# Attention and a gated network on one core: scores computed once with the queries on the partitions, probabilities transposed by TensorE, and an instruction order fixed by a list schedule

## The chip, the cores and the metric

The kernel runs on one core of a Trainium2 chip. The metric is the device time of one execution in microseconds (us). Engines are named as in the profile: PE is TensorE's matmul, PEld its weight load, DVE is VectorE, ACT is ScalarE, POOL is GpSimd, SP is the queue that issues the DMAs.

## The reference

Four batches of eight heads, 1152 keys, 64 columns a head. Neighbouring queries are averaged in pairs, which leaves 576. The heads of a batch are joined to 512 columns and go through a gated network of width 1536.

```python
q_pool = q.reshape(B, H, S // 2, 2, D).mean(axis=3)       # 4, 8, 576, 64
scores = scale * np.matmul(q_pool, k.transpose(0, 1, 3, 2))
attn = np.exp(scores - scores.max(-1, keepdims=True))
attn = attn / (attn.sum(-1, keepdims=True) + 1e-09)
x = np.matmul(attn, v)       # then (B * 576, 512)
gate = 1.0 / (1.0 + np.exp(-(x @ w_gate)))
out = (gate * (x @ w_val)) @ w_out
```

The network's weights are 64-bit floats; the kernel reads them as pairs of 32-bit words and converts them itself.

## The kernel before

To keep the accuracy of fp32 at the speed of TensorE's fp32r type, a factor is split into a rounded high half and the rest, the low half. A product is then three matmuls (high x high, high x low, low x high) that add up in PSUM; for the scores, k's halves and q's halves are stacked on the 128 partitions, 64 each, so that two matmuls do (`KA` with `QA` at L226, `KB` with `QB` at L228).

The scores are computed twice. `nat_chunk` (L186) puts the queries on the partitions and takes the maximum of each query over 384 keys at a time (L195). `aug` (L199) joins the maxima and writes them as diagonals into `QB` (L211), so that the second score pass subtracts them. That second pass, `scores` (L217), puts the keys on the partitions: for each head nine slots of 128 keys by 576 queries, cut into 256 and 320 columns (`CUT`, L28). ACT takes the exponential (L232), and the result is already the way round that the product with v needs. From head 18 on (`SPLIT`) the probabilities are split: the high half by ACT (L237), the low half by DVE (`p_lo`, L240), and the product with v is four matmuls a slot (`av`, L247); before that, v and the probabilities go in as plain fp32, with ones beside v that give the denominators. For split heads POOL adds up the exponentials (L275), and `den` (L303) sums over partitions by matmul. `av_evac`, `recip` and `norm` (L277 to L338) combine the halves, divide, and split the result x into `xh` and `xl`.

The network (`groups`, L419) is cut into thirds of the width. A group is one PSUM tile of 256 or 320 queries and 12 matmuls: 512 columns of x (L439) for the gate and the value, which give `gh` and `gl`, or 512 columns of these for the output (L469), summed into `opart`. Weights are converted once (`weight_piece`, L361, in DVE's L373, L374 and L380), split, stored in DRAM and loaded again for each batch.

Batch 0 is done in two units, first its 256, then its 320 queries, each with all eight heads; the other batches are one unit. The loop at L529 runs over slots: slot i issues the scores of i, the product with v of i - 2, and, once `ready` (L348) allows, one group of the network of the unit before. This order of the program and some priorities (`tc.high_priority`, `tc.issue_after`) go to a scheduler, which sets the order of each engine's instructions.

Of the kernel before, what the change touches and what calls it, by code (L numbers as in the profile page):

```python
# [12 lines left out]
ALU = mybir.AluOpType  # L13
PSUM = bass.MemoryType.PSUM
# [5 lines left out]

@with_exitstack
def attention_glu_kernel(ctx: ExitStack, tc: tile.TileContext, qT, kT, vt, v, wg, wv, wo, out):
# [3 lines left out]
    NC = SK // 128  # L26

    CUT = ((0, 256), (256, 576))  # L28
    FF_T = 12
    THIRDS = 3  # L30

    TURN = 15
    SPLIT = 18
    LAG = 4
    AHEAD = 2
    FIRST_W = 64

    units = [(0, (0,)), (0, (1,))] + [(b, (0, 1)) for b in range(1, B)]
    heads = [(b, ns, h) for b, ns in units for h in range(H)]
    NU = len(heads)  # L40
    NSLOT = NU * NC

    const = ctx.enter_context(tc.tile_pool(name="const", bufs=1))
    vt_p = ctx.enter_context(tc.tile_pool(name="vt", bufs=2))
    e_p = ctx.enter_context(tc.tile_pool(name="e", bufs=3))
    y_p = ctx.enter_context(tc.tile_pool(name="y", bufs=2))
    one_p = ctx.enter_context(tc.tile_pool(name="one", bufs=1))
    x_p = ctx.enter_context(tc.tile_pool(name="x", bufs=7))
    g_p = ctx.enter_context(tc.tile_pool(name="g", bufs=4))
    sg_p = ctx.enter_context(tc.tile_pool(name="sg", bufs=2))  # L50
    w_p = ctx.enter_context(tc.tile_pool(name="w", bufs=2))
    dr_p = ctx.enter_context(tc.tile_pool(name="dr", bufs=1, space=DRAM))
    ps_s = ctx.enter_context(tc.tile_pool(name="ps_s", bufs=4, space=PSUM))
    ps_a = ctx.enter_context(tc.tile_pool(name="ps_a", bufs=1, space=PSUM))
    ps_m = ctx.enter_context(tc.tile_pool(name="ps_m", bufs=2, space=PSUM))


    early = ctx.enter_context(ExitStack())
    pools = {"raw": early.enter_context(tc.tile_pool(name="raw0", bufs=2))}
    set_p = early.enter_context(tc.tile_pool(name="set0", bufs=1))  # L60

    def late_pools():
        early.close()
        pools["raw"] = ctx.enter_context(tc.tile_pool(name="raw", bufs=1))
        pools["pp"] = ctx.enter_context(tc.tile_pool(name="pp", bufs=3))
        pools["acc"] = ctx.enter_context(tc.tile_pool(name="acc", bufs=2))


    ident2 = const.tile([128, 64], F32, name="ident2")
    ones_r = const.tile([128, 192], F32R, name="ones_r")  # L70

    sets = (const, const, set_p)
    KA = [p.tile([128, SK], F32R, name=f"KA{i}") for i, p in enumerate(sets)]
    KB = [p.tile([128, SK], F32R, name=f"KB{i}") for i, p in enumerate(sets)]
    QA = [p.tile([128, SQ + 64], F32R, name=f"QA{i}") for i, p in enumerate(sets)]
    QB = [p.tile([128, SQ + 64], F32R, name=f"QB{i}") for i, p in enumerate(sets)]
    opart = [const.tile([128, SQ], F32, name=f"opart{i}") for i in range(4)]

    blk = [ones_r[:, 64:192], ones_r[:, 0:128]]

    w_d = {
        "g": dr_p.tile([FF_T, 128, 2, 2, 512], F32, name="wg_d"),
        "o": dr_p.tile([THIRDS * 4, 128, 2, 1, 512], F32, name="wo_d"),
    }

    st = {}

    def op(u):

        return u % 3 if u <= TURN else (u - TURN) % 2  # L90

    def after(u):

        if u < TURN:
            return u + 2
        return u + 1 if TURN < u < NU - 1 else None

    def split(u):
        return u >= SPLIT

    def whole(u):
        return len(heads[u][1]) == 2

    def span(u):
        ns = heads[u][1]
        return CUT[ns[0]][0], CUT[ns[-1]][1]

    def row(u):
        return heads[u][0] * H + heads[u][2]

    def less(to_vector):

        return nc.vector if to_vector else nc.gpsimd


    def load_kq(u):
        a, b = span(u)
        t = pools["raw"].tile([128, SK], F32, tag="kraw", name="kraw")
        r = pools["raw"].tile([128, 2, SQ], F32, tag="qraw", name="qraw")
        for p in (slice(0, 64), slice(64, 128)):  # L120
            nc.sync.dma_start(out=r[p, :, a:b], in_=qT[row(u)][:, :, a:b])
            nc.sync.dma_start(out=t[p], in_=kT[row(u)])
        st["kraw", u] = t
        st["qraw", u] = r

    def load_v(u):
        if split(u):
            t = pools["raw"].tile([128, NC, D], F32, tag="vraw", name="vraw")
            nc.sync.dma_start(out=t, in_=v[row(u)])
            st["vraw", u] = t  # L130
        else:

            t = vt_p.tile([128, 2, D * NC], F32, tag="vt", name="vo")
            nc.gpsimd.memset(t[:, 1 - u % 2], 1.0)
            nc.sync.dma_start(out=t[:, u % 2], in_=vt[row(u)])
            st["vt", u] = t.rearrange("p a (d c) -> p c (a d)", c=NC)


    def prep_k_hi(u):
        for s in (slice(0, SQ), slice(SQ, SK)):  # L140
            nc.scalar.activation(out=KA[op(u)][:, s], in_=st["kraw", u][:, s], func=ACTF.Copy)  # L141

    def prep_k_lo(u, part):
        s = slice(part * SQ, part * SQ + SQ)
        nc.gpsimd.tensor_tensor(  # L145
            out=KB[op(u)][64:128, s], in0=st["kraw", u][64:128, s],
            in1=KA[op(u)][64:128, s].bitcast(F32), op=ALU.subtract,
        )

    def prep_qs(u):  # L150
        a, b = span(u)
        t = pools["raw"].tile([128, SQ], F32, tag="qs", name="qs")
        qr = st.pop(("qraw", u))
        less(u == 1).tensor_tensor(out=t[:, a:b], in0=qr[:, 0, a:b], in1=qr[:, 1, a:b], op=ALU.add)
        st["qs", u] = t

    def prep_q_hi(u):
        a, b = span(u)
        for p, q in ((slice(64, 128), QB[op(u)]), (slice(0, 64), QA[op(u)])):
            nc.scalar.activation(out=q[p, a:b], in_=st["qs", u][p, a:b], func=ACTF.Copy)  # L160

    def prep_q_lo(u):
        a, b = span(u)
        less(heads[u][0] == 1).tensor_tensor(
            out=QA[op(u)][64:128, a:b], in0=st.pop(("qs", u))[64:128, a:b],
            in1=QB[op(u)][64:128, a:b].bitcast(F32), op=ALU.subtract,
        )

    def prep_v(u):
        if not split(u):  # L170
            return
        t = vt_p.tile([128, NC, 2 * D], F32R, tag="vt", name="vt")
        vr = st.pop(("vraw", u))
        nc.scalar.activation(out=t[:, :, 0:D], in_=vr, func=ACTF.Copy)
        nc.gpsimd.tensor_tensor(
            out=t[:, :, D:2 * D], in0=vr, in1=t[:, :, 0:D].bitcast(F32), op=ALU.subtract
        )
        st["vt", u] = t


    def nat_list(u):
        a, b = span(u)
        return [(t, j) for t in range(a // 128, (b + 127) // 128) for j in range(3)]

    def nat_chunk(u, t, j):
        if ("pm", u) not in st:  # L186
            st["pm", u] = y_p.tile([128, 5, 3], F32, tag="pm", name="pm")
        ps = ps_s.tile([128, 512], F32, tag="s", name="nps")
        N = 384

        nc.tensor.matmul(  # L191
            out=ps[:, 0:N], lhsT=QA[op(u)][:, t * 128:(t + 1) * 128],
            rhs=KA[op(u)][:, j * N:(j + 1) * N], start=True, stop=True,
        )
        nc.vector.tensor_reduce(  # L195
            out=st["pm", u][:, t, j:j + 1], in_=ps[:, 0:N], axis=mybir.AxisListType.X, op=ALU.max
        )

    def aug(u):  # L199
        a, b = span(u)  # L200
        t0, t1 = a // 128, (b + 127) // 128
        nm = y_p.tile([128, 5], F32, tag="nm", name="nm")
        pm = st.pop(("pm", u))
        nc.vector.tensor_reduce(
            out=nm[:, t0:t1], in_=pm[:, t0:t1], axis=mybir.AxisListType.X, op=ALU.max, negate=True
        )
        q2 = QB[op(u)][0:64, 0:SQ].rearrange("p (a c) -> p a c", c=64)
        for par in range(2):
            p = slice(64 * par, 64 * par + 64)
            n = len(range(2 * t0 + par, b // 64, 2))  # L210
            nc.vector.tensor_tensor(  # L211
                out=q2[:, 2 * t0 + par:b // 64:2], in0=ident2[p].unsqueeze(1).to_broadcast([64, n, 64]),
                in1=nm[p, t0:t0 + n].unsqueeze(2).to_broadcast([64, n, 64]), op=ALU.mult,
            )


    def scores(i):  # L217
        u, c = divmod(i, NC)
        ks = slice(c * 128, (c + 1) * 128)
        e = e_p.tile([128, SQ], F32, tag="e", name="e")  # L220
        st["e", i] = e
# [41 lines left out]
    def acc_sum(i):  # L263
        u, c = divmod(i, NC)
        a, b = span(u)
        if c == 0:
            return
# [379 lines left out]
```

## Time and profile before

| | |
|---|---|
| median of three runs | 1094.63 us (1094.1 to 1097.09) |
| the profiled execution | 1094.97 us, span 1093.2 us |
| PE busy, PEld busy | 989.4 us (91%), 937.3 us (86%) |
| DVE busy | 863.4 us (79%) |
| ACT busy, POOL busy | 636.0 us (58%), 654.7 us (60%) |
| DMA moved | 173.38 MB, mean 159 GB/s |

Busy time is a sum over instructions. A matmul's time in flight overlaps the next one's, so a PE that is busy 91% need not be at its fastest; the distance between the starts of neighbouring matmuls shows how fast they go. An idle time counts only on the engine that sets the pace of its stage. The network's first matmul starts at 104.3 us, and the last matmul of all ends some 3.5 us before the end of the span. The span runs from the first to the last instruction; the execution's time has a little more around it.

### The profile page before, as it was taken

The page shows a single profiled execution, that of the slowest core. Times are in us where ns is not written, and L with a number is a line of the kernel's source. Part 1 is how long each engine was busy: PE and PEld are TensorE (multiplying, and loading weights), DVE is VectorE, ACT ScalarE, POOL GpSimd, SP SyncE. Part 2 cuts the span into 40 slices and gives each one's busy share as a digit, 9 for nine tenths or more (in the row PEclk, how much of TensorE's full clock was granted, in tenths as well). Part 3 has the DMA queues.
Part 4 walks back from the last instruction along what each step waited for, and adds up shares of the span by engine and source line. Part 5 has one row for each costly group of instructions (what it writes and reads, how often), then busy time and mean ns, then how long its engine had stood idle before and what let it go on. Part 6 is the DMA issues. An engine that isn't in the chain of part 4 may idle for free.

```text
span 1093.2 us, 17681 instructions
## 1 busy us (share of the span) xinstructions
PE 989.4 (91%) x6328; PEld 937.3 (86%) x6328; DVE 863.4 (79%) x1310; ACT 636.0 (58%) x1413; POOL 654.7 (60%) x461
## 2 busy tenths in 40 slices
PE   4999898989999888889898898899999898999998
PEld 3889887778999878879898898888898888999998
DVE  6877989968597998989889988889989988841222
ACT  3775656565665676666676655666676555632211
POOL 5774656444466787867698767768778665620000
PEclk9999999999999998989999998999999998999999
DMA  9974876776655544544544333454434331344443
GB/s 222 290 199 110 264 233 244 239 258 208 199 184 183 170 131 132 159 129 132 142 122 131 119 113 110 132 175 127 131 105 132 111 109 40 116 160 173 146 167 98
DMA packets 46040, 173.38 MB, mean 159 GB/s; under 512 B 6016, under 2 KB 11136, under 8 KB 38272
## 3 DMA queue, kind: packets, MB, share of 16 engines
q1 hardware_dynamic: 45952, 172.25, 50.9%
q8 instruction: 50, 0.82, 0.3%
q14 instruction: 38, 0.31, 0.1%
HBM read 148.64 MB, written 23.59 MB: 158 GB/s over the span
## 4 chain that ended last, share of the span: by engine, by line
PE 44%; DVE 37%; ACT 7%; DMA 6%; issue 5%; POOL 1%; SPq 1%; DVEq 0%; ACTq 0%; POOLq 0%
PE gps L439 14%; DVE pl L243 13%; PE ops L469 10%; PE avps L258 8%; DVE pm L195 8%; PE sps L226 4%; PE sps L228 4%; DVE QB L211 3%; DVE gl L453 3%; PE nps L191 3%; ACT e L232 2%; DMA wraw<-in_wg_dram 2%; ACT ph L237 2%; DVE hh L449 2%; DVE wraw L374 1%
## 5 line engine op out<-in xcount | busy, mean ns | idle before, releaser
L439 PE MATMUL gps<-xh,wg 128*128 128x320 f32 (+1 forms) x1536 | 342.8, 302 | 2.6 <-ACT xh L336 2.4
L232 ACT ACTIVATE e<-sps 128x256 f32<-128x256 f32 (+1 forms) x576 | 220.0, 406 | 181.7 <-PE sps L228 161.1
L243 DVE TENSOR_TENSOR pl<-e,ph 128x576 fp32r<-128x576 f32 x198 | 264.1, 1339 | 38.6 <-ACT ph L237 38.0
L275 POOL TENSOR_TENSOR acc<-acc,e 128x576 f32<-128x576 f32 x148 | 238.2, 1609 | 89.7 <-ACT e L232 84.3
L195 DVE TENSOR_REDUCE pm<-nps 128x1 f32<-128x384 f32 x480 | 246.2, 546 | 34.8 <-PE nps L191 33.2
L439 PEld LDWEIGHTS gps<-xh,wg 128*128 128x128 f32 x1536 | 262.9, 194 | 3.7 <-ACT xh L336 3.0
L439 PE MATMUL gps<-xl,wg 128*128 128x256 f32 (+1 forms) x768 | 231.3, 301 | 0.0
L226 PE MATMUL sps<-QA,KA 128*128 128x256 f32 (+1 forms) x576 | 190.4, 346 | 36.5 <-DVE pm L195 31.4
L145 POOL TENSOR_TENSOR KB<-kraw,KA 64x576 fp32r<-64x576 f32 x80 | 119.9, 1500 | 109.4 <-ACT KA L141 91.1
L228 PE MATMUL sps<-QB,KB 128*128 128x256 f32 (+1 forms) x576 | 168.9, 307 | 17.3 <-DVE QB L211 17.3
L469 PE MATMUL ops<-gh,wo 128*128 128x256 f32 (+1 forms) x768 | 171.8, 302 | 2.3 <-DMA wo<-wo_d 1.6
L191 PE MATMUL nps<-KA,QA 128*128 128x384 f32 x480 | 149.5, 381 | 23.9 <-ACT KA L141 8.7
L226 PEld LDWEIGHTS sps<-QA,KA 128*128 128x128 f32 x576 | 111.5, 195 | 55.3 <-DVE pm L195 47.2
L439 PEld LDWEIGHTS gps<-xl,wg 128*128 128x128 f32 x768 | 149.1, 194 | 0.6
L237 ACT ACTIVATE ph<-e 128x576 fp32r<-128x576 f32 x198 | 135.9, 688 | 11.1 <-PE avps L258 6.3
L258 PE MATMUL avps<-e,vo 128*128 128x256 f32 (+1 forms) x360 | 136.5, 467 | 3.3 <-ACT e L232 2.3
L469 PEld LDWEIGHTS ops<-gh,wo 128*128 128x128 f32 x768 | 131.7, 194 | 3.5 <-DVE opart L480 2.0
L228 PEld LDWEIGHTS sps<-QB,KB 128*128 128x128 f32 x576 | 110.9, 196 | 24.8 <-DVE QB L211 18.6
L191 PEld LDWEIGHTS nps<-KA,QA 128*128 128x128 f32 x480 | 87.3, 197 | 35.3 <-DVE pm L195 13.2
L469 PE MATMUL ops<-gl,wo 128*128 128x256 f32 (+1 forms) x384 | 115.6, 301 | 1.6 <-DVE gl L453 1.6
L258 PEld LDWEIGHTS avps<-e,vo 128*128 128x128 f32 x360 | 100.0, 326 | 6.9 <-ACT e L232 4.4
L258 PE MATMUL avps<-pl,vt 128*128 128x256 f32 (+1 forms) x396 | 93.6, 304 | 11.7 <-DVE pl L243 11.2
(65 smaller groups left out, 1374.9 us busy)
## 6 DMA issues: line engine op xcount, KB each, us to landing
wg<-wg_d SPq DMA_DIRECT2D x48, 1024.0 KB, 4.8
wo<-wo_d SPq DMA_DIRECT2D x48, 512.0 KB, 3.3
kraw<-in_kT_dram SPq DMA_DIRECT2D x80, 288.0 KB, 4.7
qraw<-in_qT_dram SPq DMA_DIRECT2D x48, 288.0 KB, 4.7
wg_d<-wg SPq DMA_DIRECT2D x12, 1024.0 KB, 5.2
vraw<-in_v_dram SPq DMA_DIRECT2D x22, 288.0 KB, 3.6
wraw<-in_wg_dram SPq DMA_DIRECT2D x12, 512.0 KB, 5.7
wraw<-in_wv_dram SPq DMA_DIRECT2D x12, 512.0 KB, 4.9
```

The source lines that it names most:

```text
L145: nc.gpsimd.tensor_tensor(out=KB[op(u)][64:128, s], in0=st["kraw", u][64:128, s], in1=KA[op(u)][64:128, s].bitcast(F32), op=ALU.subtract,)
L191: nc.tensor.matmul(out=ps[:, 0:N], lhsT=QA[op(u)][:, t * 128:(t + 1) * 128], rhs=KA[op(u)][:, j * N:(j + 1) * N], start=True, stop=True,)
L195: nc.vector.tensor_reduce(out=st["pm", u][:, t, j:j + 1], in_=ps[:, 0:N], axis=mybir.AxisListType.X, op=ALU.max)
L226: nc.tensor.matmul(out=ps[:, 0:b - a], lhsT=KA[op(u)][:, ks], rhs=QA[op(u)][:, a:b], start=True, stop=False)
L228: st["pace"] = nc.tensor.matmul(out=ps[:, 0:b - a], lhsT=KB[op(u)][:, ks], rhs=QB[op(u)][:, a:b], start=False, stop=True)
L232: nc.scalar.activation(out=e[:, a:b], in_=ps[:, 0:b - a], func=ACTF.Exp, scale=1.0 / 16.0)
L237: nc.scalar.activation(out=t[:, a:b], in_=st["e", i][:, a:b], func=ACTF.Copy)
L243: nc.vector.tensor_tensor(out=t[:, a:b], in0=st["e", i][:, a:b], in1=st["ph", i][:, a:b].bitcast(F32), op=ALU.subtract)
L258: nc.tensor.matmul(out=ps[:, 0:b - a], lhsT=st["vt", u][:, c], rhs=s[:, a:b], start=(c == 0 and k == 0), stop=(c == NC - 1 and k == len(sr ...
L275: eng.tensor_tensor(out=t[:, a:b], in0=t[:, a:b], in1=st["e", i][:, a:b], op=ALU.add)
L439: nc.tensor.matmul(out=ps[:, 0:N], lhsT=w[:, hl, s, kc], rhs=x, start=(kc == 0 and j == 0), stop=(kc == 3 and j == 2),)
L469: nc.tensor.matmul(out=ps[:, 0:N], lhsT=w[:, hl, 0, i], rhs=x[:, qc], start=(i == 0 and j == 0), stop=(i == 3 and j == 2),)
```

## The change

Almost all of the kernel's body is replaced; the inputs, the outputs and the splitting in halves stay.

- Scores are computed once, with the queries on the partitions, over all 1152 keys: a step is 128 queries of one head, or, once in a pair of heads, the last 64 queries of both (`STEPS`). There are 9 steps a pair, 16 pairs, 144 steps. A step's scores take two and a quarter PSUM banks (`S0`; in the first 36 steps a second buffer, `S1`, alternates and takes two of the three banks of the tag `m`).
- DVE takes the maximum over 1152 columns; ACT's exponential subtracts it as a bias for each partition and sums each row on the way (`accum_out`), which gives the denominators.
- TensorE transposes the probabilities, nine blocks of 128 x 128 in three groups of three; ACT copies the high half of a group out of PSUM, DVE subtracts it from the group to get the low half.
- The product with v has 18 matmuls for 256 or 320 queries of a head. The reciprocals of the denominators are spread by POOL and transposed by TensorE.
- Batch 0 is one unit like the others. The network's products have 288 columns. High halves of k and v are made by POOL (of k's first head by ACT).
- The order comes from a list schedule in the kernel: each operation has an engine, a price, a priority and what it needs; `Plan.run` gives each free engine the ready operation with the lowest priority value, and the instructions are then issued in this order as they stand (`tc.manual_schedule`).

```diff
+class Plan:
+    LAT = {"PE": 0.22, "ACT": 0.12, "DVE": 0.12, "POOL": 0.15, "SP": 0.0}
...
+    STEPS = ((0, 0), (0, 1), (0, 2), (0, 3), (2, 4), (1, 2), (1, 3), (1, 0), (1, 1))
+    SLOTS = {
+        "S0": 1, "S1": 1, "T": 2, "m": 3, "K0": 1, "K1": 1, "Q0": 1, "Q1": 1, "qr": 1, "P": 2, "pt": 2,
+        "vr": 1, "vt": 2, "y": 2, "t": 2, "rb": 1, "x": 7, "g": 9, "opart": 8, "wg": 2, "wo": 2,
+        "cr": 2, "kr": 1, "cs": 1, "sg": 3, "den": 2,
+    }
...
+    def scores(p, j, hd, st):
...
+        cuts = ((0, 384), (384, 896), (896, SK)) if early and s % 2 else ((0, 512), (512, 1024), (1024, SK))
+        for n, (a, b) in enumerate(cuts):
+            def mm(a=a, b=b):
+                t = tl(sh)
+                seq = [(q, kk[w][:, a:b]) for w, q in lhs for kk in (KA, KB)]
+                for n, (q, k) in enumerate(seq):
+                    nc.tensor.matmul(out=t[:, a:b], lhsT=q, rhs=k, start=(n == 0), stop=(n == len(seq) - 1))
...
+        def rmax():
+            nc.vector.tensor_reduce(out=c, in_=tl(sh)[:, 0:SK], axis=AXX, op=ALU.max, negate=True)
+        def ex():
+            nc.scalar.activation(out=tl(ph), in_=tl(sh)[:, 0:SK], func=ACTF.Exp, bias=c,
+                                 accum_out=tl(st["den"])[:, col:col + 1])
...
+        for n in range(3):
+            def tr(n=n, th=th):
+                for c in range(3):
+                    k = (3 * n + c) * 128
+                    nc.tensor.transpose(out=tl(th)[:, c * 128:(c + 1) * 128], in_=tl(ph)[:, k:k + 128], identity=ident)
...
+                def hi(views=views):
+                    src, dh, dl = views()
+                    nc.scalar.activation(out=dh, in_=src, func=ACTF.Copy)
+                def lo(views=views):
+                    src, dh, dl = views()
+                    nc.vector.tensor_tensor(out=dl, in0=src, in1=dh.bitcast(F32), op=ALU.subtract)
...
+    def values(p, j, w, g, hd, st):
+                        nc.tensor.matmul(out=tl(m)[:, 0:N], lhsT=tl(hd[w]["v"])[:, c], rhs=tl(h)[:, k, c, 0:N],
+                                         start=(c == 0 and k == 0), stop=(c == NC - 1 and k == 1))
...
+    def gated(b, xs):
+        base = PB * (b + 1) + 2.5
+        step = PB / 72.0
...
+                due = PB + 12 * th - 20 + (2 * k if k < 4 else k + 4)
+                due = max(due, 6 + 2.5 * (k + 8 * th))
+                stored[kind, m_] = [convert(kind, m_, s, due) for s in range(2 if k < 4 else 1)]
...
+    order = pl.run()
+    with tc.manual_schedule():
+        for o in order:
+            o.fn()
-    def nat_chunk(u, t, j):
-    def aug(u):
-    def p_hi(i):
-    def p_lo(i):
-    def acc_sum(i):
-    def acc_split(u):
-    def den(u, n):
-    def recip(u):
```

`PB` is 36, the steps of a batch. Priorities are in steps: a step's scores, maximum and exponential have its number less 0.5, its transposes and halves its number plus 1, the network's products of batch b start at 36 (b + 1) + 2.5 and are half a step apart, and a weight piece (`convert`: load, three DVE instructions, two of ACT, one of POOL, store) has its due value. A load of converted weights has a priority 4 steps ahead of its product.

## Rows read from the trace of the kernel before

**Rows 1.** Windows by stage: length; busy PE, PEld, DVE, ACT, POOL; PE clock; DMA; GB/s

```profile
17.00:104.00 87.00, 79.35 (x360) 71.29 (x360) 67.16 (x128) 58.25 (x144) 57.42 (x55) 1.00 0.76 214
...
500.00:600.00 100.00, 94.48 (x673) 91.10 (x672) 91.25 (x124) 70.15 (x156) 80.18 (x50) 1.00 0.46 137
...
950.00:1085.00 135.00, 133.01 (x992) 132.04 (x991) 42.76 (x83) 33.67 (x79) 10.22 (x8) 1.00 0.45 151
```

**Rows 2.** The chain that ended last, share of the span by engine

```profile
PE 44%; DVE 37%; ACT 7%; DMA 6%; issue 5%; POOL 1%; SPq 1%; DVEq 0%; ACTq 0%; POOLq 0%
```

**Rows 3.** Waits: engine and line waiting, releaser; us in total, times, longest

```profile
PEld sps L226 <- DVE pm L195: 47.2, 62, 3.6
...
PEld avps L258 <- DVE pl L243: 17.4, 23, 1.4
```

**Rows 4.** Timeline of TensorE at 707 us: start, us, engine, line, instruction

```profile
706.64 0.51 PE L191 MATMUL nps<-KA,QA 128*128 128x384 f32 x2
707.00 0.28 PE L226 MATMUL sps<-QA,KA 128*128 128x256 f32 x1
...
707.23 0.31 PE L226 MATMUL sps<-QA,KA 128*128 128x320 f32 x1
...
707.52 0.28 PE L469 MATMUL ops<-gh,wo 128*128 128x256 f32 x1
```

**Rows 5.** Timeline of TensorE at 62 us, with fp32 instructions of L258

```profile
62.21 0.74 PE L258 MATMUL avps<-e,vo 128*128 128x256 f32 x2
...
62.91 0.28 PE L228 MATMUL sps<-QB,KB 128*128 128x256 f32 x1
```

**Rows 6.** Span and mean granted clock of the core

```profile
core 0: 1093.2 us, clock 0.975
```

**Rows 7.** Timeline of TensorE after a wait at 409 us

```profile
410.83 0.82 PE L228 MATMUL sps<-QB,KB 128*128 128x256 f32 x2 [2.26 <-DVE QB L211]
411.45 0.47 PE L439 MATMUL gps<-xh,wg 128*128 128x320 f32 x1
411.72 0.47 PE L439 MATMUL gps<-xl,wg 128*128 128x320 f32 x1
```

**Rows 8.** Window right behind that wait, columns as in rows 1

```profile
411.00:412.00 1.00, 1.00 (x5) 1.00 (x6) 0.97 (x2) 0.52 (x2) 0.00 (x0) 0.50 0.33 65
```

**Rows 9.** Instruction groups: line, engine, out<-in, count | busy, mean ns | idle before

```profile
L243 DVE TENSOR_TENSOR pl<-e,ph 128x576 fp32r<-128x576 f32 x198 | 264.1, 1339 | 38.6 <-ACT ph L237 38.0
...
L195 DVE TENSOR_REDUCE pm<-nps 128x1 f32<-128x384 f32 x480 | 246.2, 546 | 34.8 <-PE nps L191 33.2
L275 POOL TENSOR_TENSOR acc<-acc,e 128x576 f32<-128x576 f32 x148 | 238.2, 1609 | 89.7 <-ACT e L232 84.3
...
L232 ACT ACTIVATE e<-sps 128x320 f32<-128x320 f32 x288 | 124.0, 432 | 51.4 <-PE sps L228 48.2 <-PE avps L258 0.6
...
L232 ACT ACTIVATE e<-sps 128x256 f32<-128x256 f32 x288 | 108.2, 381 | 130.2 <-PE sps L228 112.9 <-POOL acc L275 7.4 <-POOL acc L270 3.4
...
L374 DVE SCALAR_TENSOR_TENSOR wraw<-wraw 128x512 uint32<-128x512 uint32 x36 | 33.6, 933 | 4.6 <-ACT wraw L372 3.8
L380 DVE SCALAR_TENSOR_TENSOR w<-wraw 128x512 uint32<-128x512 uint32 x36 | 33.0, 920 | 1.5
...
L373 DVE TENSOR_SCALAR wraw<-wraw 128x512 uint32<-128x512 uint32 x36 | 28.4, 789 | 9.0 <-DMA wraw<-in_wg_dram 4.5 <-DMA wraw<-in_wv_dram 3.5 <-DMA wraw<-in_wo_dram 0.7
...
L288 DVE TENSOR_TENSOR y<-avps,t 64x320 f32<-64x320 f32 x22 | 10.6, 483 | 0.2
...
L288 DVE TENSOR_TENSOR y<-avps,t 64x256 f32<-64x256 f32 x22 | 9.2, 417 | 1.3 <-ACT t L287 1.0
...
L164 DVE TENSOR_TENSOR QA<-qs,QB 64x576 fp32r<-64x576 f32 x8 | 7.1, 887 | 2.4 <-ACT QB L160 2.3
```

**Rows 10.** DMA issues: transfer, queue, count, KB each, us to landing

```profile
wg<-wg_d SPq DMA_DIRECT2D x48, 1024.0 KB, 4.8
```

**Rows 11.** The first matmul of the span

```profile
8.71 0.66 PE L191 MATMUL nps<-KA,QA 128*128 128x384 f32 x1 [8.71 <-ACT KA L141]
```

More of the change, by code (lines that the diff above doesn't have):

```diff
@@ L13, with __init__ @@
 ALU = mybir.AluOpType
+AXX = mybir.AxisListType.X
 PSUM = bass.MemoryType.PSUM
 DRAM = bass.MemoryType.DRAM
+class Op:
+    def __init__(self, eng, dur, fn, prio, after=(), take=None, late=0.0):
+        self.eng, self.dur, self.fn, self.prio = eng, dur, fn, prio
+        self.after = [a for a in after if a is not None]
+        self.take, self.late = take, late
+        self.users, self.start, self.end = [], None, None
+class Hold:
+    def __init__(self, tag, first=None):
+        self.tag, self.slot, self.ops = tag, None, []
@@ L108, in row @@
[L108 to L124, printed above, removed]
@@ L143, in prep_k_lo @@
[L143 to L155, printed above, removed]
@@ L157, in prep_q_hi @@
[L157 to L178, printed above, removed]
@@ L199, in aug @@
-    def aug(u):
[L200 to L214, printed above, removed]
@@ L369, in bits @@
         def bits():
[L371 to L372 removed]
+            low, high = tl(cr)[:, :, 0], tl(cr)[:, :, 1]
             nc.vector.tensor_scalar(out=low, in0=low, scalar1=29, scalar2=None, op0=ALU.logical_shift_right)
@@ new lines, in hi, with lo, store @@
+        def hi():
+            nc.scalar.activation(out=tl(cs)[:, 0], in_=tl(cr)[:, :, 0].bitcast(F32), func=ACTF.Copy)
+        def lo():
+            nc.gpsimd.tensor_tensor(out=tl(cs)[:, 1], in0=tl(cr)[:, :, 0].bitcast(F32),
+                                    in1=tl(cs)[:, 0].bitcast(F32), op=ALU.subtract)
+        def store():
+            nc.sync.dma_start(out=w_d[kind][m][:, :, s], in_=tl(cs).bitcast(F32))
+        a = pl.op("SP", dma(512), load, due - 4, take=[cr], late=3.0)
+        a = pl.op("ACT", act(512), scale, due, after=[a], uses=[cr])
@@ L612, in attention_glu_kernel, with store @@
-    post()
+                            nc.vector.scalar_tensor_tensor(out=o, in0=ps, scalar=0.5, in1=o, op0=ALU.mult, op1=ALU.add)
+                    if th == 0:
+                        a = pl.op("ACT", act(HALF), post, at - 1, after=[last], uses=[ms], take=[oh])
+                    else:
+                        a = pl.op("DVE", dve(HALF), post, at - 1, after=[last, prev], uses=[ms, oh])
+                    acc[dm, n][1] = a
+                    if th == 2:
+                        def store(dm=dm, n=n, oh=oh):
+                            c = b * SQ + n * HALF
+                            nc.sync.dma_start(out=out[dm * 128:(dm + 1) * 128, c:c + HALF], in_=tl(oh))
+                        pl.op("SP", dma(144), store, at, after=[a], uses=[oh], late=3.0)
@@ new lines, in attention_glu_kernel @@
+    in_turn = []
+    acc = {}
+    xs = {}
+    blocked = [pl.hold("m"), pl.hold("m")]
+    pl.op("SP", 0.0, lambda: None, -100, take=blocked)
+    for b in range(B):
+        for p in range(4 * b, 4 * b + 4):
+            st = {}
+            hd = [head_operands(2 * p, p * NS), head_operands(2 * p + 1, p * NS + 4)]
+            for j in range(NS):
+                scores(p, j, hd, st)
+                for jj, w, g in ((1, 0, 0), (4, 0, 1), (6, 1, 1), (8, 1, 0)):
+                    if j == jj:
+                        values(p, j, w, g, hd, st)
+            xs[p] = normalise(p, st)
+        if b == 0:
+            for th in range(3):
+                for k in range(8):
+                    kind, m_ = ("wg", 4 * th + k) if k < 4 else ("wo", 4 * th + k - 4)
+                    due = PB + 12 * th - 20 + (2 * k if k < 4 else k + 4)
+                    due = max(due, 6 + 2.5 * (k + 8 * th))
+                    stored[kind, m_] = [convert(kind, m_, s, due) for s in range(2 if k < 4 else 1)]
+        gated(b, [xs[4 * b + k] for k in range(4)])
```

834 lines of the change are left out of this document (414 added, 420 removed).

## The prediction, made before the changed kernel was run

> **What bounds the kernel now.** I read the busy time by stage first, then the chain of waits, then the costliest groups. TensorE has a matmul in flight for nearly all of each stage [rows 1], but in the 500 to 600 us stage DVE is 91% busy too, while from 950 to 1085 us, where only the gated network runs, DVE is at 32% and TensorE at 99% [rows 1]. The chain that ended last gives PE 44% and DVE 37% [rows 2]. So most of the middle is a race between two engines: TensorE waits for DVE's maxima and for the low halves of the probabilities [rows 3], and for the diagonal of maxima written by L211 [rows 7].
>
> How full TensorE really is comes from start-to-start distances, not from busy time: the 256-column matmuls follow each other at about 0.119 us, 320 columns at 0.146, 384 columns at 0.18 [rows 4]: 0.012 us plus 0.00042 us a column. An fp32 multiplication by `vo` counts double: its two instructions and one 256-column matmul take 62.21 to 62.91, so 0.29 us each [rows 5]. The work before is then: scores 1152 x 0.1325 = 153; maxima 480 x 0.173 = 83; gated network 3456 x 0.1325 = 458; split attention-value products 792 x 0.1325 = 105; fp32 ones 360 x 0.31 = 112; denominators 88 x 0.1325 = 12. Sum 923 us of a 1093 us span. The mean granted clock of 0.975 [rows 6] means 5% of the span at 1.2 GHz, which costs some 27 us; the other 143 us are gaps. One gap shows both: TensorE waits 2.26 us for L211 and 320 columns then take 0.27 us [rows 7], at a granted clock of 0.50 [rows 8].
>
> **What the change does to each engine.** TensorE. The second, untransposed score pass (83 us) goes, and so do the fp32 products and the denominators. Scores: an ordinary step is 2 x (512 + 512 + 128 columns) = 4 x 0.227 + 2 x 0.066 = 1.04 us, the shared step of a pair twice that, so 10.4 us a pair of heads, 166 in all. Attention-value products: 72 a pair at 0.1325, 153 us. Gated network: 3456 of 288 columns at 0.133, 460 us. New are 81 + 5 transposes a pair, 1376 in all, and no row shows one. Below: a 128-column matmul on the line above, 0.066 us. Above: the fp32 instruction's 0.29. I take 0.12: the nearest row in kind is a weight load of 128 columns with its matmul, and the smallest distance that the trace shows for such a pair is 0.119 [rows 4]. That gives 165 us (91 to 399). Sum 944, which is no less than before: the change frees no TensorE time, it must win by filling gaps.
>
> The Trainium skill speaks against this price ("TensorE: Matmul & The Clock Gate", Part 4: PE-mode transpose): it tells of some 275 ns for one in a kernel's context. By that the transposes would take 378 us and TensorE's sum would be 1157; no run here shows one yet.
>
> DVE. A maximum over 1152 columns from PSUM: 0.546 + 768 x 0.00103 = 1.34 us (the slope between the two L288 rows, which read PSUM too [rows 9]); 12.0 us a pair. The low halves now read PSUM. Before, both operands lay in SBUF and one took 1.34 us on the mean; the PSUM-reading additions of L288 take 0.417 and 0.483 for 256 and 320 columns [rows 9], so 384 columns take 0.55 and 192 take 0.35: 24 x 0.55 + 6 x 0.35 = 15.3 us a pair. With the four additions (1.8), normalisation (1.6) and the low queries (2 x 0.89 [rows 9]) a pair costs 32.5 us, 3.6 a step. All 16: 520, against 246 + 264 + some 65 for L211 and the rest before. To it come 36 weight pieces at 0.789 + 0.933 + 0.920 = 2.64 [rows 9], 95 us, and 160 PSUM reads of 288 columns at 0.45, 72 us. Sum 687 against 863.
>
> ACT. An exponential of 1152 columns by the two L232 rows (0.0008 us a column) is 0.432 + 832 x 0.0008 = 1.10 [rows 9]. What summing a row on the way costs is not shown: between nothing and another fixed part of an instruction, 0.381 - 256 x 0.0008 = 0.18; at most 25 us in all, on an engine that stays under 60%. Three high-half copies of 384 columns (0.48 each) make 1.45. With tanh and the copies 3.9 us a step, beside 6.5 on TensorE. POOL loses the running sums of L275 and gets k's high halves; at the 1.61 us of an L275 sum [rows 9] for each of some 18 full-width instructions in nine steps, and 24 short ones a batch, it is busy some 35 us of 58: hidden. DMA: k for 32 heads, not 40; the 48 + 48 weight loads stay. It moves a little less in a little less time, under the 214 GB/s that 17 to 104 us showed [rows 1]. SP waits in the plan's order: a weight load stands behind the store of its converted piece and behind older ones, and is issued four steps ahead of use, some 20 us against a landing of 4.8 [rows 10].
>
> **The end, by stages.** (1) The first 36 steps are batch 0's attention with no gated network under it: before, half of the queries came first and the network began at about 104 us; now all queries of batch 0 come first. TensorE's work there is a quarter of 166 + 165 + 153, 121 us, so it does not bind. DVE does: 4 x 32.5 = 130, plus the pieces due by step 36. The due values in the diff (first third from 16 to 27, second from 28 on) put 20 or 21 pieces there, 55 us. 185 us at a 95% fill, after 8 us until the first operands are in (the first matmul before began at 8.71 [rows 11]): 203 us. (2) What is left is bound by TensorE: 944 - 121 = 823 us. A step is 3.4 us of attention and two products of 12 x 0.133, 6.5 in all. DVE needs 3.6 + 0.5 a step and, for the first 15 to 18 steps, 2.2 more for the 15 late pieces: 6.3, just under. The single score buffer cycles through 1.04 + 1.34 + 1.10 to 1.3 and three hand-overs of 0.2 to 0.3, by estimate 4.3 us, so there are 2 us of slack in which TensorE multiplies for the network; behind a score matmul that waits too long stand all the planned products, since each queue is fixed. The transposed blocks' two buffers go round in three groups of 1.9 us over two, 2.8 us. Fill: the pure network stage held 992 matmuls of about 0.1325 in 135 us, 97% [rows 1], and 673 with a mean of 0.137 gave 92% from 500 to 600 us. I take 97% for the last 115 us and 96.5% before: 823 / 0.966 = 852. (3) Last evacuation and store: 3.5 us as now. Span 203 + 852 + 4 = 1059; the profiled execution took 1094.97 for its span of 1093.2, so 1.8 more: 1061 us, beside the median of 1094.63 (the profiled run is 0.3 above it).
>
> **Rivals.** (B) A transpose's weight load is hidden and the pair takes 0.066. 1032 transposes lie behind step 36: 1032 x 0.054 / 0.966 = 58 us less, 1003. For it: 256, 320 and 384 columns lie on one line [rows 4], so nothing says that 0.119 is a floor set by the load. Against it: no pair under 0.119 is seen. (C) A transpose runs as the fp32 rows do: 1032 x (0.29 - 0.12) / 0.966 = 182 us more, 1243, slower. For it: the data is plain fp32, as `e` was [rows 5]. Against it: moving data needs no several-part product. The point from which it decides: 33 us more / 1032 x 0.966, a price of 0.15 a transpose. The 275 ns of the Trainium skill ("TensorE: Matmul & The Clock Gate", Part 4: PE-mode transpose) fall on this side and would give about 1227. (D) The fixed order stalls TensorE: each queue waits where the plan's prices are wrong, a wait of about 2 us is followed by a half clock [rows 7, 8], and the fill falls to the 91% that a busy middle stage has today: 823 / 0.91 = 904, 1113. It loses to today's kernel from 823 / 888, a fill below 92.7%. Against it: tight hand-overs (scores, transposes) are some 6 of 16 pieces a step, and the products beside them have no fresh input. (E) The opening is worse: all 36 pieces are done before step 36 because they fill every gap, 15 x 2.64 = 40 us more there, of which little comes back: 1101. (F) The opening runs at half clock: its TensorE is busy 121 us of 195 and every third microsecond of that is transposes; at the 0.50 of [rows 8] the 121 become 242, TensorE binds the opening, which ends at 250, and the kernel at 1108. Against it: the opening of now keeps 1.00 [rows 1]. It is what the Trainium skill says of transposes ("TensorE: Matmul & The Clock Gate", Part 4: PE-mode transpose), that they do not bring the full clock; no run here shows it. (G) Nothing is won: what the gaps give back the opening takes, 1094.
>
> **Chances.** Forecast 0.50, by itself 1035 to 1088 (opening 189 to 215, fill 95 to 98%); B 0.18; C 0.10; D 0.11; E 0.05; F 0.02; G 0.04. About 0.3% is what a measurement of this kernel can tell from no change. Faster 0.71 (forecast, B and the mild ends of D and E), same 0.06, slower 0.23. The range goes from B with a quick opening, 985, to D and E, 1120, and leaves out C and the far ends.
>
> **What would show it.** The start-to-start time of three transposes in a row: 0.12 right, 0.066 B, over 0.15 C. The first gated matmul at 200 to 215 us: right; 240 or more: E or F, by the granted clock. The windows from there to the last 120 us: granted clock of 0.97 or more and a fill of 96%: right; many 1.2 GHz stretches and score or transpose matmuls that wait for exponentials: D. DVE should fall to about 690 us, near full only in the first 200. The prediction is wrong if the first stage is not bound by DVE, or if the later one is bound by anything but TensorE.

## The result, and the profile after

The changed kernel takes 1058.2 us (median of 4 runs, 1057.66 to 1058.91) against 1095.44: a ratio of 0.966, interval 0.9643 to 0.9676. 1061 was forecast. The time came out as predicted; its two large parts did not, and their errors cancel.

The page of the changed kernel, span and busy time, with the granted clock in 40 slices:

```profile
span 1056.2 us, 18322 instructions
...
PE 981.1 (93%) x6944; PEld 931.3 (88%) x6944; DVE 654.6 (62%) x1086; ACT 561.3 (53%) x1179; POOL 423.7 (40%) x408
...
PEclk9889988999999999999999999999999999999999
```

Busy PE is 8 us shorter than before, DVE 209 us. Windows of the same profile, columns as in [rows 1]: the opening up to the first gated matmul, the stage with attention and network, the network alone.

```profile
10.00:226.00 216.00, 159.37 (x908) 134.10 (x908) 169.16 (x260) 131.07 (x262) 108.89 (x95) 0.91 0.56 157
226.00:927.00 701.00, 696.27 (x5096) 672.49 (x5096) 461.00 (x771) 401.15 (x854) 291.29 (x282) 1.00 0.51 158
927.00:1056.00 129.00, 124.85 (x945) 124.41 (x943) 23.47 (x53) 25.90 (x60) 20.80 (x25) 1.00 0.45 151
```

```profile
L541 PE MATMUL bank<-x,wg x2304: 288/295/404, 226.6 to 1038.6; 128*128 128x288 f32 x192
```

The last row gives the network's first matmul: 226.6 us. Up to there no engine is full: PE 74%, DVE 78%, at a mean granted clock of 0.91. From there on TensorE is busy 99% and the clock is 1.00, the upper of its two levels. The chain that ended last (by engine, then by line) tells the same; [rows 2] had PE 44% and DVE 37%:

```profile
PE 76%; DVE 3%; ACT 1%; issue 1%; DMA 0%; ACTq 0%; DVEq 0%
PE bank L541 43%; PE bank L326 12%; PE bank L408 11%; PE bank L367 10%; PE bank L455 1%; DVE cr L503 1%; DVE cr L498 1%; DVE pt L386 1%; DVE nm L333 1%; ACT P L338 0%; ACT pt L382 0%; DVE cr L497 0%; DMA wo<-wo_d 0%; ACT cr L493 0%; DVE sg L581 0%
```

Pieces of TensorE's timeline at 600 us and in the network's own stage, columns as in [rows 4]:

```profile
601.18 0.40 PE L326 MATMUL bank<-KA,Q 128*128 128x512 f32 x1
601.41 0.39 PE L326 MATMUL bank<-KB,Q 128*128 128x512 f32 x1
...
602.12 0.49 PE L367 MATMUL bank<-ident,P 128*128 128x128 f32 x3
602.36 0.31 PE L326 MATMUL bank<-KA,Q 128*128 128x128 f32 x1
602.50 0.28 PE L326 MATMUL bank<-KB,Q 128*128 128x128 f32 x1
602.62 1.81 PE L541 MATMUL bank<-g,wo 128*128 128x288 f32 x12
604.26 0.49 PE L367 MATMUL bank<-ident,P 128*128 128x128 f32 x3
604.51 1.03 PE L541 MATMUL bank<-g,wo 128*128 128x288 f32 x6
605.38 0.49 PE L367 MATMUL bank<-ident,P 128*128 128x128 f32 x3
...
1029.83 9.05 PE L541 MATMUL bank<-x,wg 128*128 128x288 f32 x67
1038.72 6.51 PE L541 MATMUL bank<-g,wo 128*128 128x288 f32 x48
```

A network matmul among others takes 0.133 us (67 in 8.89 us, 1029.83 to 1038.72), 512 columns 0.23. From the first of three transposes to the matmul behind them pass 0.25 us (604.26 to 604.51), which would be 0.083 each. But this next matmul starts early and pays for it: the six network matmuls from 604.51 to 605.38 take 0.87 us and not 6 x 0.133 = 0.80. Together the three transposes and the six take 1.12 us; less 0.80 this leaves 0.32, so a transpose costs 0.11. In the same way, from 602.12 to 604.26 three transposes, two score matmuls of 128 columns and twelve network matmuls take 2.14 us; less 12 x 0.133 this leaves 0.54 for five, 0.11 each, for the 128-column matmuls too and not 0.066.

The groups that answer to [rows 9]:

```profile
L367 PE MATMUL bank<-ident,P 128*128 128x128 f32 x1296 | 214.1, 280 | 34.4 <-DVE pt L386 31.4 <-ACT P L338 2.8
L386 DVE TENSOR_TENSOR pt<-bank,pt 128x384 fp32r<-128x384 f32 x384 | 203.9, 550 | 103.6 <-ACT pt L382 101.8
L333 DVE TENSOR_REDUCE nm<-bank 128x1 f32<-128x1152 f32 x144 | 195.1, 1355 | 63.4 <-PE bank L326 60.4 <-ACT P L338 2.2
...
L338 ACT ACTIVATE P<-bank,nm 128x1152 f32<-128x1152 f32 x144 | 175.8, 1221 | 50.5 <-DVE nm L333 43.0 <-PE bank L326 5.5 <-DVE cr L497 1.9
...
L503 DVE SCALAR_TENSOR_TENSOR cr<-cr 128x512 uint32<-128x512 uint32 x36 | 34.5, 958 | 1.0
...
L386 DVE TENSOR_TENSOR pt<-bank,pt 128x192 fp32r<-128x192 f32 x96 | 29.3, 350 | 19.1 <-ACT pt L382 18.8
...
L338 ACT ACTIVATION_READ_ACCUMULATOR P<-bank,nm 128x1 f32 x144 | 28.6, 198 | 0.0
...
L497 DVE TENSOR_SCALAR cr<-cr 128x512 uint32<-128x512 uint32 x36 | 23.4, 649 | 2.5 <-DMA cr<-in_wg_dram 1.4 <-DMA cr<-in_wo_dram 0.9
```

The low halves, once 1.34 us for 576 columns with both operands in SBUF, take 0.550 us for 384 columns reading PSUM; the last section shows what made the former so long. The maximum of 1152 columns takes 1.355 (1.34 was worked out).

### The profile page after: what moved, and what is told of

The parts are those of the page before. It is cut to its first block, busy times and chain, and to the rows that moved or that the text cites. A ratio compares the mean times of both kernels' runs of the same rounds, so it can differ in the third digit from the quotient of the medians.

```text
span 1056.2 us, 18322 instructions
## 1 busy us (share of the span) xinstructions
PE 981.1 (93%) x6944; PEld 931.3 (88%) x6944; DVE 654.6 (62%) x1086; ACT 561.3 (53%) x1179; POOL 423.7 (40%) x408
## 4 chain that ended last, share of the span: by engine, by line
PE 76%; DVE 3%; ACT 1%; issue 1%; DMA 0%; ACTq 0%; DVEq 0%
PE bank L541 43%; PE bank L326 12%; PE bank L408 11%; PE bank L367 10%; PE bank L455 1%; DVE cr L503 1%; DVE cr L498 1%; DVE pt L386 1%; DVE nm L333 1%; ACT P L338 0%; ACT pt L382 0%; DVE cr L497 0%; DMA wo<-wo_d 0%; ACT cr L493 0%; DVE sg L581 0%
## 5 line engine op out<-in xcount | busy, mean ns | idle before, releaser
L541 PE MATMUL bank<-x,wg 128*128 128x288 f32 x2304 | 369.4, 303 | 0.0
L541 PEld LDWEIGHTS bank<-x,wg 128*128 128x128 f32 x2304 | 316.2, 188 | 0.1
L386 DVE TENSOR_TENSOR pt<-bank,pt 128x384 fp32r<-128x384 f32 (+1 forms) x480 | 233.1, 510 | 122.6 <-ACT pt L382 120.7
L382 ACT ACTIVATE pt<-bank 128x384 fp32r<-128x384 f32 (+1 forms) x480 | 206.9, 460 | 121.3 <-PE bank L367 115.1
L367 PE MATMUL bank<-ident,P 128*128 128x128 f32 x1296 | 214.1, 280 | 34.4 <-DVE pt L386 31.4
L333 DVE TENSOR_REDUCE nm<-bank 128x1 f32<-128x1152 f32 x144 | 195.1, 1355 | 63.4 <-PE bank L326 60.4
L326 PE MATMUL bank<-KA,Q 128*128 128x512 f32 (+3 forms) x480 | 177.5, 371 | 27.9 <-ACT P L338 12.5
L338 ACT ACTIVATE P<-bank,nm 128x1152 f32<-128x1152 f32 x144 | 175.8, 1221 | 50.5 <-DVE nm L333 43.0
L541 PE MATMUL bank<-g,wo 128*128 128x288 f32 x1152 | 183.8, 303 | 1.3 <-DMA wo<-wo_d 1.3
L408 PE MATMUL bank<-pt,vt 128*128 128x256 f32 (+1 forms) x1152 | 168.8, 301 | 0.0
```

The source lines that it names most:

```text
L326: nc.tensor.matmul(out=t[:, a:b], lhsT=q, rhs=k, start=(n == 0), stop=(n == len(seq) - 1))
L333: nc.vector.tensor_reduce(out=c, in_=tl(sh)[:, 0:SK], axis=AXX, op=ALU.max, negate=True)
L338: nc.scalar.activation(out=tl(ph), in_=tl(sh)[:, 0:SK], func=ACTF.Exp, bias=c, accum_out=tl(st["den"])[:, col:col + 1])
L367: nc.tensor.transpose(out=tl(th)[:, c * 128:(c + 1) * 128], in_=tl(ph)[:, k:k + 128], identity=ident)
L382: nc.scalar.activation(out=dh, in_=src, func=ACTF.Copy)
L386: nc.vector.tensor_tensor(out=dl, in0=src, in1=dh.bitcast(F32), op=ALU.subtract)
```

## The experiments

"Opening" means the time of the first gated matmul. A time without a range is that of a single run. The kernel before came at 1091.0 to 1092.6 us beside these runs and at 1095.4 beside the changed kernel, so 4 us and less between two of the times below say nothing. Line numbers shift by one or two where an edit adds lines.

The first question was why the opening took 226.6 us and not 203. Three theories: A, the two score buffers S0 and S1 share PSUM bank 2 and wait for each other's readers; B, DVE's load; C, the two T buffers of the transposed blocks go round too slowly. What TensorE waits for from 20 to 200 us in the changed kernel (us in total, times, longest) has something of C and A; the first row fits B as well, because the low halves stand in DVE's queue:

```profile
PE bank L367 <- DVE pt L386: 22.1, 18, 3.8
PE bank L326 <- ACT P L338: 10.3, 12, 2.5
PE bank L326 <- DVE nm L333: 6.0, 9, 0.9
...
```

**No conversion on DVE.**

```diff
...
-        a = pl.op("DVE", 2 * dve(512), bits, due, after=[a], uses=[cr])
-        a = pl.op("DVE", dve(512), join, due, after=[a], uses=[cr])
```

> Left out: the three DVE instructions that turn a 64-bit weight into 32 bits (ACT copies the high word as it stands), and their entries in the plan. The opening (up to the first gated matmul, 226.6 us in the changed kernel) holds 16 of the 36 pieces, 42 us of DVE. Theory B, the opening is set by DVE's load: first gated matmul near 190, time 1020 to 1030. Theory A (the two score buffers are tied to each other by the PSUM bank that they share) and theory C (the two buffers of the transposed blocks go round too slowly): first gated matmul no earlier than 214, time over 1045. After the opening no gain under any of them, because TensorE binds there.

Measured: opening 205.8, time 1033.29. This lies between the theories: 42 us of DVE work taken away give 21 back. DVE is then busy only 66% of the window from 10 to 200 us, and still the opening is 206:

```profile
10.00:200.00 190.00, 150.10 (x865) 124.96 (x865) 126.04 (x202) 125.16 (x253) 97.61 (x91) 0.95 0.61 173
```

**One score buffer.**

```diff
-        early = s < PB
+        early = False
```

> The opening uses the score buffer S0 alone, as the rest of the kernel does, and the network's three banks are free from the start. Theory A: S1 shares bank 2 with S0 and each waits for the other's readers, so the second buffer brings little; opening within 10 us of 226, time 1050 to 1070. Theory C says the same. If S1 works as a real second buffer, a step becomes a chain of scores, maximum and exponential of 4.3 us plus queueing: opening 20 to 50 us longer, time 1080 to 1110.

Measured: opening 236.8, time 1071.94. S1 is worth 10 us of opening, at the upper end of what A allowed.

**Score buffers apart, one T buffer.**

```diff
-        "S1": [bank[:, SK:2 * SK]],
...
+        "S1": [bank[:, 1536:1536 + SK]],
...
-        block = [] if not early else [blocked[0], blocked[1]]
+        block = [] if not early else blocked
...
-    blocked = [pl.hold("m"), pl.hold("m")]
+    blocked = [pl.hold("m"), pl.hold("m"), pl.hold("T")]
```

> S1 is moved to banks 3 to 5, apart from S0; in the opening one T buffer is left. Theory A: score matmuls no longer wait for the other buffer's readers; opening 185 to 210. Theory C: the transposed blocks go round one buffer three times a step, 3 x 1.85 us = 5.6 us plus queueing, so the opening grows to 250 or more and the time to 1080 or more. Theory B: no change from the move itself.

Measured: opening 290.4, time 1119.64, as C said. Two things were changed at once, so what the score buffers gain by lying apart is not seen here. TensorE's wait for the low halves, which free the T buffer, grows from 22 to 54 us:

```profile
PE bank L367 <- DVE pt L386: 53.7, 43, 2.9
...
```

**One score buffer, four T buffers.**

```diff
+        "TE": [bank[:, 512 * i:512 * i + 512] for i in (3, 4)],
...
+        sh, ph = pl.hold("S0"), pl.hold("P")
...
-            th = pl.hold("T")
+            th = pl.hold("TE" if early and (3 * s + n) % 2 else "T")
```

> In the opening one score buffer and four T buffers (banks 3, 4, 6, 7) in place of two and two; the rest as it was. Theory C: the transposes no longer wait for the low halves; opening 180 to 200, time 1015 to 1035. Theory A: as with one score buffer, within 10 us of 226. Theory B: within 5 us of 226, as DVE's work is the same.

Measured: opening 225.3, time 1058.56. The waits for T are gone, and those for the score buffer (ACT's exponential has to read it) have taken their place:

```profile
PE bank L327 <- ACT P L339: 42.8, 23, 3.9
...
PE bank L368 <- DVE pt L387: 1.4, 2, 0.9
```

With one score buffer, two more T buffers take the opening from 236.8 to 225.3; with the T buffers as they were, S1 takes it from 236.8 to 226.6. So C is not the sole cause either: PSUM moved from one ring to the other moves the wait with it. (A ring is a buffer that is written, read by one or two engines, and only then free for the next writer.) B's forecast, no change for the same DVE work, was met as well; this run alone does not separate A from B.

**Transposes twice.**

```diff
-                for c in range(3):
+                for c in [0, 1, 2] * (1 if early else 2):
```

> After the opening every probability block is transposed twice into the same PSUM columns; plan and order as in the changed kernel. 972 more transposes at the 0.083 us that three in a row show. If TensorE binds the rest of the kernel (the prediction): 81 us more, time 1130 to 1145, first gated matmul still at 226. If the chain through ACT and DVE bound it, the transposes would go into waits: less than 25 us more. If a transpose really costs the 0.12 of the prediction: 117 us more.

Measured: 1159.22, span 1157.4, opening 226.5: 101 us more for 972 transposes, 0.104 each. TensorE does bind the long stage. The price of one more lies between the two numbers that were named, because 0.083 leaves out what the next matmul pays. Six transposes and six network matmuls take 1.45 us here (603.04 to 604.49), where three and six took 1.12: 0.33 for three more, 0.11 each.

```profile
603.04 0.82 PE L367 MATMUL bank<-ident,P 128*128 128x128 f32 x6
603.61 1.04 PE L541 MATMUL bank<-x,wg 128*128 128x288 f32 x6
604.49 0.82 PE L367 MATMUL bank<-ident,P 128*128 128x128 f32 x6
```

**Maximum twice.**

```diff
-            nc.vector.tensor_reduce(out=c, in_=tl(sh)[:, 0:SK], axis=AXX, op=ALU.max, negate=True)
+            for _ in range(1 if early else 2):
+                nc.vector.tensor_reduce(out=c, in_=tl(sh)[:, 0:SK], axis=AXX, op=ALU.max, negate=True)
```

> After the opening DVE takes every maximum twice, 108 x 1.355 = 146 us more of DVE work; plan and order unchanged. If TensorE binds with slack in the step's chain (the prediction counted 2 us a step): less than 8 us more. If the chain of scores, maximum and exponential had no slack: 1.36 us a step, up to 146 us more.

Measured: 1126.61, 68 us more, where the prediction's slack allowed 8. DVE was not full (busy 524 us of the 670 from 230 to 900 us), so the slack that the prediction counted was not there for the running kernel.

**Maximum twice, and the plan told.** The same kernel with one more edit:

```diff
-        a = pl.op("DVE", dve(SK), rmax, ...
+        a = pl.op("DVE", dve(SK) * (1 if early else 2), rmax, ...
```

> The maximum is taken twice after the opening as in the run before (68 us more, where the prediction had counted 2 us of slack a step), but now the plan is told the doubled price, so the order is laid out for it. Theory: the slack is there for the plan and gone once the order is fixed, because TensorE meets the next score or transpose just when the plan expects its input; then this costs less than 20 us, time 1058 to 1080, with TensorE without waits again. Rival: the chain of a step has no room for 1.36 us more; then 50 to 80 us as before, time 1105 to 1140.

Measured: 1078.55, 20 us more than the changed kernel, the upper edge of what was expected, and 48 less than with the same work in an order laid out for the old price. TensorE's waits shrink, but not to those of the changed kernel. They are, from 230 to 900 us, in the changed kernel, with the maximum twice, and with the plan told:

```profile
PE bank L367 <- DVE pt L386: 3.6, 3, 1.5
PE bank L455 <- DVE sg L581: 1.2, 1, 1.2
```

```profile
PE bank L368 <- DVE pt L387: 21.8, 30, 2.8
PE bank L326 <- ACT P L339: 13.9, 31, 1.3
...
```

```profile
PE bank L368 <- DVE pt L387: 10.9, 13, 2.0
PE bank L326 <- ACT P L339: 3.2, 5, 1.6
...
```

So most of the slack belongs to the plan. In a fixed order TensorE comes to the next transpose or score when the plan expects its input, and a step that is longer than planned is waited for.

**The kernel before, without its first pass.**

```diff
     def nat_chunk(u, t, j):
+        return
     def aug(u):
+        return
...
+        nc.vector.memset(QB[i][0:64, 0:SQ].bitcast(F32), 0.0)
```

> The kernel before, without its first score pass: L191, its maxima on DVE and the diagonals are left out and nothing is subtracted from the scores. TensorE loses 83 us of work, DVE some 312. Race theory (the prediction: TensorE waits for DVE in the middle): time 900 to 960, more than TensorE's own 83 us. Rival, TensorE alone bound the kernel before: 1005 to 1020. Rival, the middle was bound by other waits (low halves, weights): over 1030.

Measured: 947.14, some 144 us less than the 1091.0 of the kernel before beside it. The race was real: 83 us of TensorE and some 312 of DVE taken away give 144, more than TensorE's share. How much of the other 61 us is DVE's load, and how much the wait for the diagonals that hang on the maxima, was not tried apart. With the maximum left out altogether, the old order runs at 93% busy PE:

```profile
span 945.3 us, 16067 instructions
...
PE 875.0 (93%) x5848; PEld 843.8 (89%) x5848; DVE 655.3 (69%) x713; ACT 612.1 (65%) x1413; POOL 686.1 (73%) x461
```

**S1's shared columns last.**

```diff
-        cuts = ((0, 384), (384, 896), (896, SK)) if early and s % 2 else ...
+        cuts = ((384, 896), (896, SK), (0, 384)) if early and s % 2 else ...
```

> S1's scores are computed with the columns in the shared bank 2 last and not first; same plan, same order. Theory A: score matmuls of S1 wait less for the readers of S0; first gated matmul 5 to 20 us earlier, time 1040 to 1053. Rival (T buffers and DVE's queue set the opening, as the runs with one and four T buffers suggest): within 4 us of 226 and of 1058.

Measured: 1054.83 (1053.52 to 1056.22), ratio 0.9664, interval 0.9626 to 0.9702, opening 224.6. The waits for DVE's maximum at the score matmuls fall from 6.0 to 0.4 us, and next to nothing comes of it, as the rival said. The ratio is that of the changed kernel (0.966). A is there, and is worth 2 us of the opening at most: with the plan told of the doubled maximum, an edit that acts behind the opening, it was 224.6 too.

**Prices changed.** (`B2` stands for the shared bank, held from the matmul that writes it to the exponential.)

```diff
-    T_PE = 0.12
+    T_PE = 0.083
-        return n / 2400 + 0.013
+        return max(n / 2400 + 0.0145, 0.115)
...
+        "B2": [None],
...
```

> Only what the plan believes is changed: a transpose 0.083 us in place of 0.12, matmuls 1.5 ns more, 128 columns 0.115, the DVE instructions of a weight piece 2.56 in place of 2.05, the low queries 1.1 in place of 0.75, and the bank that the two score buffers share counted as one resource. If wrong prices cost the fixed order time: 1035 to 1050, the opening 5 to 15 us shorter. If the opening is what its engines and buffers allow whatever the plan believes: within 5 us of 1058.

Measured: 1046.4 (1044.88 to 1049.31), ratio 0.9574, interval 0.953 to 0.9618, opening 217.0: both within what was expected if wrong prices cost the order time. Not every new price is truer: 0.115 for 128 columns is near the 0.11 of the rows above, but a transpose's 0.083 lies farther below them than 0.12 lay above. Which of the changes gave the 12 us was not tried apart.

**Prices and priorities.**

```diff
...
-            a = pl.op("PE", 3 * T_PE, tr, s + 1 + 0.1 * n, after=[ex_op], uses=[ph], take=[th])
+            a = pl.op("PE", 3 * T_PE, tr, s + 0.5 + 0.1 * n, after=[ex_op], uses=[ph], take=[th])
-                    due = max(due, 6 + 2.5 * (k + 8 * th))
+                    due = max(due, 6 + 3 * (k + 8 * th)) + 3
-        base = PB * (b + 1) + 2.5
+        base = PB * (b + 1) + 4
```

> As the run before, and: S1's columns in the shared bank last; transposes and halves half a step earlier in priority (s + 0.5), maximum and exponential s - 0.8; weight pieces due later (6 + 3 (k + 8 th) + 3 at least); the network's products 1.5 steps later. Theory: the transposed blocks' two buffers and DVE's queue set the opening together, so taking the halves first frees the buffers sooner and moves pieces into the later stage, where DVE is at 60%: first gated matmul 200 to 215, time 1025 to 1045. Rival: no order helps; within 5 us of the run with prices alone.

Measured: 1018.1 (1016.26 to 1019.46), ratio 0.9306, interval 0.9271 to 0.934. It beats both kernels. The opening is 191.2, earlier than expected, and the time lies below the range. Same buffers, same 16 converted pieces up to there, about the same DVE work (164 us for 169), but DVE is now 91% full (164.14 of 181), and the clock is 0.96:

```profile
10.00:191.00 181.00, 145.69 (x905) 124.20 (x905) 164.14 (x261) 132.59 (x263) 112.41 (x95) 0.96 0.66 189
191.00:900.00 709.00, 708.52 (x5195) 686.38 (x5196) 470.16 (x783) 402.25 (x858) 293.43 (x282) 1.00 0.52 158
```

```profile
L543 PE MATMUL bank<-x,wg x2304: 288/295/383, 191.2 to 999.1; 128*128 128x288 f32 x192
```

```profile
L505 DVE SCALAR_TENSOR_TENSOR cr<-cr x16: 631/684/1669, 14.6 to 181.4; 128x512 uint32<-128x512 uint32 x16
```

**Four T buffers and no conversion.** One score buffer, four T buffers, and the conversion's DVE instructions left out, as in the two runs above.

> The opening with one score buffer and four T buffers (225 us by itself) and without the three DVE instructions of a weight piece (206 us by itself); left out is the conversion of the weights. If DVE's queue and the T buffers are two limits in series, together 185 to 198 and a time of 1010 to 1025. If the one score buffer is now the limit (its waits rose to 54 us in the run with four T buffers): 203 to 215, no better than without the conversion alone, time 1030 to 1045.

Measured: opening 209.2, time 1035.72, no better than without the conversion alone. The longest wait is that for the single score buffer:

```profile
PE bank L327 <- ACT P L339: 33.2, 21, 3.0
...
```

DVE's queue still counts beside it: four T buffers with the conversion had 225.3, so leaving it out gave 16 us here too.

What the opening is made of, as I read these runs: the rings of score buffers and T buffers and DVE's queue are about equally tight, and each run that eased one met the next. What eased them together was the order. Prices alone gave 10 us, prices and priorities 35; which of the priorities did it was not tried apart.

## Why the prediction was right, and where it was not

*TensorE frees no time.* Held: the sum of 944 stands, because two terms of it were off by about the same in opposite directions. A transpose costs 0.11 us, not 0.12, so the 1376 take 151 us, 14 less than counted. A score matmul of 128 columns costs 0.11 too, not the 0.066 of the line, which makes 14 us more for 320 of them. The prediction named both values for the same pair, a weight load and 128 columns: it took 0.066 for the scores and something near the right price for the transposes. Against the 923 us of before TensorE has some 20 us more to do; the gain is all gaps and clock.

*The stage bound by TensorE.* Held, but for one term: the fill. 852 us and an end of 4 were forecast, 829.6 us pass from the first gated matmul to the end. With the same two corrections the work stays near the 823 us that were counted, and it stands in 826: TensorE is busy 99% of that time, where a fill of 96.6% was taken. That term is most of the 26 us. Doubled transposes show that it is TensorE's time that counts there.

*The opening bound by DVE.* This step failed, and with it the prediction's own condition that the first stage be bound by DVE. 203 was forecast, 226.6 measured. 16 pieces were converted, not 21, and DVE had less to do than the 185 us counted (169), but it was 78% full, not 95%. The prediction looked at the rings of the buffers in the later stage only; the runs put the rings of the score and T buffers, in the order that the plan had fixed, beside DVE's queue in the opening. With better priorities DVE does fill to 91%, and the opening then falls below the forecast.

*The number.* That 1058.2 lies 3 us from 1061 is luck: an opening 24 us too long and a later stage 26 us too short. Both lie outside the bounds that went with the forecast (opening 189 to 215, fill 95 to 98%).

*Two us of slack a step.* Failed as a statement about the running kernel: 1.36 us more on DVE cost 0.63 a step, and 0.19 once the plan was told. The prediction took slack from a sum of durations, which says what a planner can do, not what a fixed order will.

*DVE.* 687 us were worked out, 654.6 are measured; the PSUM-reading prices from the L288 rows [rows 9] held to about 1%. *ACT.* Summing a row shows as an instruction of its own, 198 ns in flight and 28.6 us in all, just above the bounds given (0.18 each, 25 in all).

*Rivals.* B (0.066) and C (0.15 or more) are both out; the price, 0.11, lies just under the forecast's. D, the stall of a fixed order, is a real mechanism, as the doubled maximum shows, but in the changed kernel's long stage TensorE waited under 5 us. (The point from which D loses is 823 / 885 by the prediction's own sum, not 823 / 888; nothing hangs on it.) E foresaw a worse opening, by more converted pieces; it was worse with fewer. F: the opening's clock was 0.91, not 0.50, and 0.96 in the run that filled it better; in the long stage, with some ten transposes a step, it was 1.00.

The Trainium skill's 275 ns ("TensorE: Matmul & The Clock Gate", Part 4: PE-mode transpose) agrees with the mean time in flight here, 280 ns; as a price of one transpose in a row of them it would be two and a half times too high. That transposes do not bring the full clock (same section) no run here shows: the stage below 1.00 is the opening, in which TensorE is busy 74%, and whether its transposes have a part in that was not tried.

## What to carry to other kernels

In a fixed order, slack counts only if the planner knows the true durations: measure them, put them in, and plan again after every change of a duration. Where no engine is full, as in the opening here, look which buffer each wait frees, expect the next ring behind the first, and try priorities before memory. And price an operation neither by its time in flight nor by the distance to the next start alone, but by what it adds to a whole stretch, the next instructions included.

## What the runs showed of the hardware that was not expected

- A transpose of 128 x 128 fp32 costs 0.11 us among matmuls, while one has a time in flight of 0.28. In a group of three they start 0.109 us apart; the matmul behind starts 0.03 us after the last, and its own successor comes 0.08 us later than usual. So the distance from the group's first start to the next start, 0.25 us, is about a quarter short.
- A weight load with a matmul of 128 columns costs the same 0.11 us, hardly less than the 0.119 of 256 columns [rows 4], and not the 0.066 that the line through the wider ones gives.
- L503, a DVE instruction with both operands in SBUF, took between 0.68 and 1.80 us in the opening: it waits for a GpSimd instruction that is already running. L386 (384 columns) and L333, which read PSUM, always take nearly the same; L386 0.55 us whether POOL was running as it began or idle throughout.

```profile
L503 DVE SCALAR_TENSOR_TENSOR cr<-cr x16: 681/694/1803, 16.9 to 218.1; 128x512 uint32<-128x512 uint32 x16
```

```profile
167.99 1.84 POOL L262 TENSOR_TENSOR qr<-qr 128x576 f32<-128x576 f32 x1
...
168.61 1.77 DVE L503 SCALAR_TENSOR_TENSOR cr<-cr 128x512 uint32<-128x512 uint32 x1
```

  In these rows of the timeline at 168 us L503 ends 0.55 us behind POOL's instruction (170.38, 169.83). So it is in the whole trace of the changed kernel: the 15 of L503 that began while POOL ran an instruction ended 0.55 to 0.57 us behind that instruction's end, and the 21 others, with POOL idle or starting later, took 0.68 to 0.70. The low halves of before, with both operands in SBUF, spread alike:

```profile
L243 DVE TENSOR_TENSOR pl<-e,ph x198: 689/1428/2016, 300.8 to 961.7; 128x576 fp32r<-128x576 f32 x198
```

  The 15 of them beside which POOL ran nothing took 0.74 on the mean. By that estimate some 118 of DVE's 863 us before, 198 x (1.34 - 0.74), went into such waits. The low halves of the changed kernel read PSUM: 480 of them, for all heads and not only from head 18 on, take 233 us where the 198 took 264.

  The Trainium skill ("GPSIMD Engine Reference", 1. Specifications) says that GpSimd shares VectorE's way to SBUF, and that the two contend where a DVE instruction has two SBUF inputs or runs in a two-port mode. These rows agree with that; no run here took GpSimd's work away. L497, with one SBUF input, spreads too (0.42 to 1.64), and no row tells in which mode it ran.
